# Linear attention gated by an MLP mixer: the first loads in the order in which the products take them up, and other planner settings

## The chip, the cores and the metric

The kernel runs on one core of one Trainium2 chip. The metric is the device time of one execution in microseconds; the median of the runs is compared. TensorE is called PE in the profile, VectorE DVE, ScalarE ACT, GpSimd POOL, and SyncE, which here issues most of the DMAs, SP.

## The reference

x is a 2048x512 float32 matrix (one batch). Its layer norm feeds two branches, and the output is x + s*g:

```python
xn = layernorm(x)
# A: linear attention, H = 32 heads of 16
q, k, v = heads(xn @ wqkv)
phi = lambda t: where(t > 0, t + 1, exp(t)) + 1e-6
pq, pk = phi(q), phi(k)
kv  = einsum("bhsd,bhse->bhde", pk, v)
z   = einsum("bhsd->bhd", pk)
o   = einsum("bhqd,bhde->bhqe", pq, kv) / (einsum("bhqd,bhd->bhq", pq, z)[..., None] + 1e-6)
s   = o.reshape(B, S, D) @ wo
# B: spatial-shift mixer and MLP, D = 512, F = 1376
h  = gelu(layernorm(xn) @ w1)
hs = (four quarters of h's columns, shifted by +1, -1, +2, -2 tokens) @ w2
x1 = xn + hs
g  = silu(x1 + gelu(layernorm(x1) @ w3) @ w4)
out = x + s * g
```

## The kernel before

**Arithmetic.** Nearly every float32 product is split: an operand a is written as a_h + a_l, each of a 32-bit type that PE takes at one pass (fp32r), and a product becomes three matmuls, a_h b_h, a_l b_h and a_h b_l. The ending h or l in a tile's name says which part it is. ACT makes the high part (a copy with a conversion), DVE the low part (a subtraction). A few small products are done as slow float32 matmuls. The weights of the key and query projections have their mean over the rows taken out; the sums for that are the tiles wkt and wqt, and ksum and wqm are the products with ones that come out of them.

**Stages.** x is cut into 16 row blocks of 128 tokens (x0, x1, ...; the tile's name in the profile is x) and, transposed, into 4 blocks of 512 tokens of four 128-row chunks each (xt, whose split parts are u). The first stage projects keys (k, weights wk) and queries (q, weights wq) of a block of 512 tokens. For each row block, sums of x and of its squares (sq, sx, mv on ACT and DVE), a chain of four small POOL operations (w, rs, ns, nm), the normalized x on ACT, and the nonlinearity of k (kt, kr on ACT and DVE, k0h its high part) lead to the Gram products g<-k0h,x0h, which gather keys and values over all tokens. Further stages mix the tokens, then go through the MLP in four blocks of 512 tokens (products into pb, pe, acc), with the attention (products s<-m_b..,q0h), a gate and the output after each block. The products of the mixer and the MLP are arranged in a scheme with seven products in place of eight.

**Order.** A class `Plan` records every operation with its engine, a duration, its tiles and its predecessors. The helpers that record are `mm` (line L146 in the profile), `act` (L167), the DVE and POOL helpers (L189, L194, L199), `load` (L205), `store` (L210), `fetch` (L217) and `gather` (L223, an accumulating DMA on the POOL queue). So all matmuls of the kernel have one line, and an operation is told by its tiles. `emit` then writes one order of instructions for each engine, by a list scheduling over the durations of a model:

- `deadlines` gives the PE operations nominal times in the order in which they were recorded. `backward` walks back from consumers to producers: a producer is due when its earliest consumer is, less a gap and its own duration; for a DMA the duration is an allowance of 6.0 us plus 4 us per MB.
- An operation that reads PSUM off PE is due at its own earliest time plus `PATIENCE` at the latest.
- `nudged` moves single operations ahead: the table `SOONER` lists pairs of an operation's number and a count of quarter microseconds. The operations 19 to 37 are among the first loads and their conversions.
- `emit` takes, among the ready operations of an engine, the one that is due first. `lead` bounds how early a buffer of a pool may be taken before its operation is due (pool "w" holds weights), `window` how far PE may run ahead of its nominal order, and `ahead` the same for a product that opens a new PSUM buffer.

The order is then fixed: an instruction waits on semaphores for its inputs, and everything behind it on its engine waits too. DMAs that SP issues share eight completion semaphores, so SP's ninth DMA waits for the landing of its first.

Of the kernel before, what the change touches and what calls it, by code (L numbers as in the profile page):

```python
# [85 lines left out]
class Plan:  # L86
# [138 lines left out]


    GAP = .06
    PATIENCE = 5.0
    COLD, COLD_TILL = 1.84, 5.8
    SAFE = 2.0  # L230
    early = 0.0
# [8 lines left out]
    def deadlines(self, first):  # L240
# [8 lines left out]
        for op in self.ops:  # L249
# [3 lines left out]
            elif any(t.psum for t in op.tiles):  # L253
                op.due = min(op.due, op.at + self.PATIENCE)
            elif op.soon:
# [5 lines left out]
    def backward(self):  # L261
        for op in reversed(self.ops):
            if op.eng != "PE":
                for o in op.post:
                    op.due = min(op.due, o.due - self.GAP - (6.0 + op.mb * 4 if op.mb else op.lat))

    def emit(self, first, lead, reserve, window, ahead, table=()):
        self.deadlines(first)
# [125 lines left out]
def linear_attn_gated_by_mixer(  # L394
# [43 lines left out]
    pl = Plan(nc, pools, counts, ("acc", "mm"))  # L438
# [904 lines left out]
    for b in range(NQ):  # L1343
# [50 lines left out]
        else:  # L1394
# [17 lines left out]
                gate(b * QT + QT - 1, a, o, D // 2, late=True, by_dma=False, whole=o > 0)  # L1412

    SOONER = (
# [5 lines left out]
    )  # L1420
    pl.emit(first=6.0, lead={"p": 12.0, "w": 10.0, "ab": 10.0}, reserve={"p": 20, "w": 1, "ab": 0}, window=6.0,
            ahead=6.0, table=SOONER)


# [35 lines left out]
```

## Time and profile before

| | |
|---|---|
| median of 3 runs | 521.98 us (521.84 to 522.37) |
| profiled execution | 522.82 us |
| its span in the trace | 520.8 us |
| PE busy | 513.3 us (99%) |
| DVE, ACT, POOL busy | 375.4, 330.7, 110.5 us |
| granted clock of PE | 1.0 throughout |
| HBM traffic | 60.33 MB read, 30.81 MB written |
| chain that ended last | PE 90%, ACT 3%, DMA 3%, DVE 2% |

The profiled execution is 2.02 us longer than its span, and 0.84 us above the median. Rows of the timeline give the start in us from the beginning of the span, the duration, the engine, the helper's line, the operation, the tiles (out<-in, without their buffer numbers), the shapes, and in brackets the idle time before the instruction with what ended it. Durations of matmuls overlap, so PE's pace is read from the distance between starts. A row of SPq is the issue of a DMA, not its transfer. Rows of waits give the total, the number and the longest.

### The profile page before, as it was taken

The numbers are of one execution on the slowest core, as the hardware profiler recorded it, in microseconds if no ns is written. First come the engines' busy times: TensorE is split into PE (matmuls) and PEld (weight loads), VectorE is DVE, ScalarE is ACT, GpSimd is POOL, SyncE is SP. The second block draws the span as 40 slices with busy tenths as digits, with TensorE's granted clock in tenths as the row PEclk, the third lists the DMA queues.
The fourth block names the chain that finished last, engine by engine and source line by source line (L and its number), as shares of the span: only waits on it lengthen the run. The fifth ranks groups of instructions, "written<-read, shape, count | busy, mean of one in ns | idle before, by whom it ended". The sixth has DMA issues, their size and how long they took to land.

```text
span 520.8 us, 8908 instructions
## 1 busy us (share of the span) xinstructions
PE 513.3 (99%) x3017; PEld 446.4 (86%) x3017; DVE 375.4 (72%) x746; ACT 330.7 (63%) x667; POOL 110.5 (21%) x207
## 2 busy tenths in 40 slices
PE   8999999999999999999999999999999999999996
PEld 6777888988888888898999889899898898999985
DVE  4975787668555847999997558896668767695635
ACT  5799884578757858769766656366563456545621
POOL 2478313330463032212000022000140000320000
PEclk9999999999999999999999999999999999999999
DMA  7939993374897279999765769748399465797704
GB/s 269 276 85 203 241 246 79 81 164 141 171 246 188 82 170 247 247 244 264 260 234 188 223 172 225 249 155 192 110 183 299 147 198 129 158 288 232 282 2 119
DMA packets 73281, 100.12 MB, mean 192 GB/s; under 512 B 7844, under 2 KB 30900, under 8 KB 73236
## 3 DMA queue, kind: packets, MB, share of 16 engines
q1 hardware_dynamic: 62148, 79.37, 48.6%
q0 software_dynamic: 11088, 20.19, 23.4%
q8 instruction: 23, 0.38, 0.3%
q14 instruction: 22, 0.18, 0.1%
HBM read 60.33 MB, written 30.81 MB: 175 GB/s over the span
## 4 chain that ended last, share of the span: by engine, by line
PE 90%; ACT 3%; DMA 3%; DVE 2%; issue 0%; SPq 0%; POOL 0%; POOLq 0%; DVEq 0%
PE acc L146 22%; PE pb L146 10%; PE h L146 9%; PE g L146 8%; PE k L146 7%; PE q L146 7%; PE pe L146 5%; PE pbm L146 4%; PE pbs L146 3%; PE pa L146 2%; PE pem L146 2%; PE s L146 2%; PE pes L146 2%; PE a L146 2%; DMA xo<-x1d 2%; PE pam L146 1%
## 5 line engine op out<-in xcount | busy, mean ns | idle before, releaser
L223 POOL DMA_DIRECT2D xo<-x1d x12 | 10.7, 1158 | 168.5 <-ACT xo L167 114.0
L223 POOL DMA_DIRECT2D o<-x x16 | 14.5, 904 | 62.2 <-DVE o L189 44.0
L223 POOL DMA_DIRECT2D th<-in_x x14 | 12.2, 934 | 71.3 <-DVE th L199 57.7
L167 ACT ACTIVATE p<-pb 128x256 f32<-128x256 f32 x20 | 7.7, 384 | 26.3 <-PE pb L146 25.9
L223 POOL DMA_DIRECT2D pqd<-qe x16 | 14.4, 899 | 40.7 <-ACT qe L167 23.4
L199 DVE SCALAR_TENSOR_TENSOR kr<-kt,kr 128x512 f32<-128x512 f32 x16 | 11.1, 691 | 14.5 <-ACT kt L167 14.5
L167 ACT ACTIVATE gf<-gf 128x256 f32<-128x256 f32 (+1 forms) x40 | 20.9, 523 | 0.9
L199 DVE SCALAR_TENSOR_TENSOR kt<-wneg,mv,k 128x512 f32<-128x512 f32 x16 | 11.9, 746 | 10.1 <-PE k L146 9.9
L223 POOL DMA_DIRECT2D zacc<-kr x16 | 15.2, 949 | 14.0 <-DVE kr L199 8.5
L167 ACT ACTIVATE th<-xo 128x512 f32<-128x512 f32 (+1 forms) x16 | 9.6, 615 | 13.1 <-DVE xo L189 11.8
L167 ACT ACTIVATE ht<-ht 128x512 f32<-128x512 f32 x16 | 9.8, 629 | 12.4 <-DVE ht L189 12.4
L189 DVE TENSOR_TENSOR ht<-h,abc 128x512 f32<-128x512 f32 x16 | 10.8, 686 | 8.8 <-PE h L146 6.7
L189 DVE TENSOR_TENSOR gf<-pa,p 128x256 f32<-128x256 f32 x20 | 8.4, 421 | 11.0 <-PE pa L146 5.4
L167 ACT ACTIVATE p<-pe 128x256 f32<-128x256 f32 x20 | 7.6, 381 | 12.9 <-PE pe L146 12.9
L167 ACT ACTIVATE x<-x,nm,rs 128x512 f32<-128x512 f32 x16 | 12.3, 804 | 5.5 <-POOL nm L189 5.5
L167 ACT ACTIVATE y<-o,nm,rs 128x512 f32<-128x512 f32 x16 | 11.9, 805 | 3.8 <-POOL nm L194 3.8
L590 DVE BATCH_NORM_STATS2 st<-o 128x6 f32<-128x512 f32 x16 | 11.0, 686 | 4.6 <-DMA o<-x 4.6
L189 DVE TENSOR_TENSOR gf<-u,pe 128x256 f32<-128x256 f32 x20 | 8.3, 415 | 7.8 <-PE pe L146 7.8
L167 ACT ACTIVATE qe<-q,ns 128x512 f32<-128x512 f32 x16 | 10.9, 679 | 4.6 <-PE q L146 4.5
L167 ACT ACTIVATE kr<-kt,rs 128x512 f32<-128x512 f32 x16 | 11.5, 716 | 2.7 <-DVE kt L199 2.7
L199 DVE SCALAR_TENSOR_TENSOR qz<-pq,zb 128x512 f32<-128x512 f32 x16 | 10.8, 681 | 2.6 <-PE acc L146 2.6
L199 DVE SCALAR_TENSOR_TENSOR th<-th,so 128x512 f32<-128x512 f32 (+1 forms) x17 | 10.9, 657 | 2.2 <-ACT th L167 1.6
(1569 smaller groups left out, 2190.7 us busy)
## 6 DMA issues: line engine op xcount, KB each, us to landing
w_s<-in_w SPq DMA_DIRECT2D x28, 256.0 KB, 6.2
x<-in_x SPq DMA_DIRECT2D x16, 256.0 KB, 4.9
zacc<-kr POOLq DMA_DIRECT2D x16, 256.0 KB, 5.4
pqd<-qr SPq DMA_DIRECT2D x16, 256.0 KB, 3.0
pqd<-qe POOLq DMA_DIRECT2D x16, 256.0 KB, 5.0
o<-x POOLq DMA_DIRECT2D x16, 256.0 KB, 5.4
x1d<-o SPq DMA_DIRECT2D x16, 256.0 KB, 3.7
pq<-pqd SPq DMA_DIRECT2D x16, 256.0 KB, 3.8
```

The costliest lines, as they stand in the source:

```text
L146: lambda: nc.tensor.matmul(out.get(), lhs.get(), rhs.get(), start=start, stop=stop, skip_group_check=more))
L167: nc.scalar.activation(out.get(), src.get(), func, scale=get(scale), **kw)
L189: self.vec(eng, out, [a, b], lambda: self.e(eng).tensor_tensor(out.get(), a.get(), b.get(), op=op), True)
L199: lambda: self.nc.vector.scalar_tensor_tensor(out.get(), a.get(), get(s), b.get(), op0=op0, op1=op1),
L223: lambda: self.nc.gpsimd.dma_start(out.get(), get(src), accum_op=ALU.add), mb=mb)
L590: pl.add("DVE", .62, .69, [xv], [st], lambda: nc.vector.bn_stats(st.get(), xv.get()))
```

## The change

The same operations are recorded, and only the planner's settings differ: `PATIENCE` is halved, the DMA allowance in `backward` falls from 6.0 to 4.0 us, `window` is doubled, `ahead` falls from 6.0 to 4.0, the lead of the weight pool grows from 10 to 14, and the table `SOONER` is another one, with large entries for the first loads.

```diff
-    PATIENCE = 5.0
+    PATIENCE = 2.5
...
-                    op.due = min(op.due, o.due - self.GAP - (6.0 + op.mb * 4 if op.mb else op.lat))
+                    op.due = min(op.due, o.due - self.GAP - (4.0 + op.mb * 4 if op.mb else op.lat))
...
     SOONER = (
-        19, 6218, 23, 5332, 27, 842, 30, 870, 34, 216, 36, 863, 40, 23, 42, 842, 44, 606, 45, 153, 129, 10,
-        137, 641, 139, 89, 143, 41, 183, 55, 185, 178, 187, 92, 189, 92, 191, 14, 362, 5, 625, 6, 632, 15,
...
+        19, 13683, 20, 10270, 21, 8588, 23, 12463, 26, 10287, 28, 89, 29, 8809, 31, 9, 32, 8315, 34, 248,
+        35, 9622, 37, 16, 42, 972, 44, 621, 45, 262, 55, 85, 83, 60, 91, 24, 93, 19, 129, 21, 137, 828, 139, 77,
...
     )
-    pl.emit(first=6.0, lead={"p": 12.0, "w": 10.0, "ab": 10.0}, reserve={"p": 20, "w": 1, "ab": 0}, window=6.0,
-            ahead=6.0, table=SOONER)
+    pl.emit(first=6.0, lead={"p": 12.0, "w": 14.0, "ab": 10.0}, reserve={"p": 20, "w": 1, "ab": 0}, window=12.0,
+            ahead=4.0, table=SOONER)
```

Each engine runs as many instructions as before. The new orders differ in about 95 rows on PE, 226 on DVE, 145 on ACT, 36 on POOL and 83 on SP, most of them moved by a few places. The first loads on SP:

| place | before | after |
|---|---|---|
| 1 | wk, chunk 0 (256 KB) | wk, chunk 0 |
| 2 | xt chunk 0, first half (128 KB) | xt chunk 0, first half |
| 3 | xt chunk 0, second half (128 KB) | xt chunk 1 |
| 4 | xt chunk 2 (256 KB) | wk, chunk 1 |
| 5 | wk, chunk 1 (256 KB) | xt chunk 0, second half |
| 6 | xt chunk 1 (256 KB) | xt chunk 2 |
| 7 | x0 (256 KB) | wk, chunk 2 |
| 8 | wk, chunk 2 (256 KB) | xt chunk 3 |
| 9 | xt chunk 3 (256 KB) | x0 |
| 10 | wk, chunk 3 (256 KB) | wk, chunk 3 |

On PE the products of chunk 1 for the first two row blocks come right behind the float32 ones of chunk 0; on ACT two second passes of sq (row blocks 2 and 3) stand ahead of k1h, and qe and qr of the first row blocks behind k2h. The last 60 rows of PE are the same in both.

7 rows, old and new, of the table SOONER are left out of this document.

## The prediction

> **What bounds the kernel now.** I read the page first, then what PE waits for, then the busy time by stretch, then single instructions where PE is not full.
>
> ```profile
> PE 513.3 (99%) x3017; PEld 446.4 (86%) x3017; DVE 375.4 (72%) x746; ACT 330.7 (63%) x667; POOL 110.5 (21%) x207
> ...
> PE k L146 <- ACT u_1h L167: 0.7, 1, 0.7
> PE g L146 <- ACT k2h L167: 0.4, 1, 0.4
> ...
> 5.00:10.00 5.00, 4.18 (x13) 2.51 (x14) 3.13 (x6) 3.00 (x7) 0.00 (x0) 1.00 0.92 312
> ...
> 30.00:40.00 10.00, 9.57 (x42) 7.48 (x41) 6.58 (x17) 9.87 (x19) 7.82 (x15) 1.00 0.43 102
> ```
>
> The first line says that TensorE is busy in 513.3 of 520.8 us. The next two are the longest waits in the middle of its work, both in the first 40 us. The stretches confirm it: PE lacks 0.82 us between 5 and 10 and 0.43 us between 30 and 40, and in the second of these it is ACT that is full (9.87 of 10). The change issues the same operations, so PE's work stays as it is, and only the places where PE stands still, or runs at less than its pace, can give or cost time. PE's order is a single queue, so whatever it loses at one place stays lost unless a later wait absorbs it.
>
> ```profile
> 8.28 0.40 PE L146 MATMUL k<-wk_0h,u_0l 128*128 128x512 f32 x1
> 9.42 0.50 PE L146 MATMUL k<-wk_1h,u_1h 128*128 128x512 f32 x1 [0.74 <-ACT u_1h L167]
> ...
> 20.00 0.73 PE L146 MATMUL g<-k0h,x0h 128*128 128x512 f32 x2
> ...
> 29.30 0.40 PE L146 MATMUL q<-wq_1h,u_1h 128*128 128x512 f32 x1
> 29.54 1.20 PE L146 MATMUL g<-k1h,x1h 128*128 128x512 f32 x4
> ...
> 35.20 0.40 PE L146 MATMUL q<-wq_1l,u_1h 128*128 128x512 f32 x1
> 36.02 1.20 PE L146 MATMUL g<-k2h,x2h 128*128 128x512 f32 x4 [0.43 <-ACT k2h L167]
> ```
>
> A 512-wide product takes PE one step of about 0.23 us (29.30 to 29.54 is 0.24; the longer durations of the rows overlap). By that step three places can be priced: 8.28 to 9.42 is 1.14, less 0.23 makes 0.91 us lost for u_1h; 35.20 to 36.02 is 0.82, less 0.23 makes 0.59 us lost for k2h; 29.30 to 29.54 loses nothing.
>
> **The first loads.** The change swaps the order on SP. Before: weight chunk 0, two halves of token chunk 0, token chunk 2, weight chunk 1, token chunk 1, row block x0, weight chunk 2, token chunk 3. After: weight chunk 0, half of token chunk 0, token chunk 1, weight chunk 1, the other half, token chunk 2, weight chunk 2, token chunk 3, and x0 only as the ninth.
>
> ```profile
> 7.37 0.33 SPq L205 DMA_DIRECT2D wq_s<-in_wqkv  x1
> 8.73 0.33 SPq L205 DMA_DIRECT2D x<-in_x  x1
> 9.35 0.33 SPq L205 DMA_DIRECT2D wq_s<-in_wqkv  x1
> ...
> 11.12 0.33 SPq L205 DMA_DIRECT2D x<-in_x  x1
> ```
>
> SP has eight loads under way and issues another when the one eight places back has landed, so its late issues date the landings: the issue at 7.37 dates the fifth load (weight chunk 1), at 8.73 the sixth (token chunk 1), at 9.35 the seventh (x0), at 11.12 the ninth (token chunk 3). All carry 256 KB but the two halves of 128 KB, and I take it that a load lands when as many bytes have come in ahead of it as before. Token chunk 1 is then complete with 640 KB in place of 1280 KB, well before 7.37 and not at 8.73; weight chunk 1 with 896 KB in place of 1024, some 0.7 us sooner (estimate: half of the 1.36 us between 7.37 and 8.73 that 256 KB took). x0 comes ninth, so it lands at about 11.1 in place of 9.35: 1.8 us later. PE's order follows: products of chunks 0 and 1 first, in the order in which they come.
>
> The 0.91 us for u_1h go. What is late next: the second half of chunk 0, which now comes fifth and lands where weight chunk 1 did, at about 7.4; weight chunk 1's conversion on ACT; and the sum over the weights, whose last addition on DVE now stands behind x0's row sums. I give the waits for them 0.2 us each, 0.6 in all (bounds 0.3 and 1.0). The first 45 products come out ahead by 0.3 us.
>
> **Row block 0.** g<-k0h at 20.00 is the first consumer of a chain that begins with x0.
>
> ```profile
> 9.36 0.64 ACT L167 ACTIVATE sq<-x 128x512 f32<-128x512 f32 x1
> ...
> 14.42 0.81 ACT L167 ACTIVATE x<-x,nm,rs 128x512 f32<-128x512 f32 x1 [1.73 <-POOL nm L189]
> ...
> 17.00 0.71 ACT L167 ACTIVATE kr<-kt,rs 128x512 f32<-128x512 f32 x1
> ...
> 19.22 0.72 ACT L167 ACTIVATE k0h<-kr,tiny 128x512 fp32r<-128x512 f32 x1 [0.76 <-DVE kr L199]
> ...
> 25.50 0.62 ACT L167 ACTIVATE u_0h<-xt 128x512 fp32r<-128x512 f32 x1
> 26.02 0.73 ACT L167 ACTIVATE kr<-kt,rs 128x512 f32<-128x512 f32 x1
> ...
> 28.78 0.71 ACT L167 ACTIVATE k1h<-kr,tiny 128x512 fp32r<-128x512 f32 x1
> 29.39 0.71 ACT L167 ACTIVATE sq<-x,sx 128x512 f32<-128x512 f32 x1
> 30.10 0.71 ACT L167 ACTIVATE sq<-x,sx 128x512 f32<-128x512 f32 x1
> ...
> 35.26 0.71 ACT L167 ACTIVATE k2h<-kr,tiny 128x512 fp32r<-128x512 f32 x1
> ```
>
> ```profile
> 11.40 0.62 POOL L194 TENSOR_SCALAR w<-mv 128x1 f32<-128x1 f32 x1 [8.35 <-DVE mv L194]
> ...
> 13.91 0.47 POOL L189 TENSOR_TENSOR nm<-mv,ns 128x1 f32<-128x1 f32 x1
> ...
> 25.08 0.24 POOL L194 TENSOR_SCALAR w<-mv 128x1 f32<-128x1 f32 x1 [3.70 <-DVE mv L194]
> ...
> 26.61 0.19 POOL L189 TENSOR_TENSOR nm<-mv,ns 128x1 f32<-128x1 f32 x1
> ```
>
> From sq at 9.36 to the normalized x at 14.42 the chain took 5.06 us, of which four tiny POOL operations took 11.40 to 14.38, 2.98 us. The same four for the next rows took 25.08 to 26.80, 1.72 us. With x0 at 11.12, x is normalized from about 16.2 at the long price and from 14.9 at the short one. Before, kr could start only at 17.00, and x ends by 17.0 even at the long price, so the chain of x0 eats its slack but hardly passes it. The change also puts x0h behind kr and kt on ACT, which takes one conversion out of the way of k0h (0.52 us, 25.50 to 26.02). g<-k0h comes between 19.2 (short price: x0h's 0.52 and PE's lead of 0.3 both tell) and 20.1 (long price: kr at 17.0 as before); I take 19.6, near the middle, since nothing in the trace of before has these operations beside each other: 0.4 us ahead.
>
> A page of the Trainium skill speaks against the short price: "SBUF — State Buffer", section "Who interferes with whom", says that a VectorE instruction with two inputs in SBUF and a GpSimd instruction that reads SBUF shut each other out for the whole instruction. By it the long price would hold, because VectorE's order in the changed kernel has such instructions (the weight sums, the low halves) all through this stretch. The two stretches of POOL rows are what the rule would give; that the first ran beside such VectorE work I take as the cause, but no run shows it yet. I make it a rival below.
>
> **Row blocks 1 and 2.** On ACT two second passes of the row sums (sq of blocks 2 and 3) move from behind k1h to ahead of it, u_0h of the next tokens moves from ahead of it to later, and kr, kt, x, x2h, k2h follow k1h directly, with the q conversions (qe, qr) behind them.
>
> k1h is pushed back by 2 x 0.71 and pulled forward by u_0h's slot (25.50 to 26.02, 0.52): 0.90 us later, less the 0.4 by which row block 0 is ahead. It starts at 29.28, ends at 29.99, and g<-k1h starts at 30.0. PE by then has two more q products behind it (2 x 0.23 = 0.46), which makes 30.0 worth 29.54: the gain up to here is nil, and a new wait of some 0.4 us for k1h shows. From k1h's start to k2h's ACT then takes what kr to k1h took, 28.78 - 26.02 = 2.76, and a slot of k1h more (0.61), so k2h is ready at about 33.4. g<-k2h stands five q products earlier, at 36.02 - 0.59 - 5 x 0.23 = 34.3 plus nothing gained: its wait of 0.59 us goes, with 0.9 us to spare. The conversions of q that are now later must be read before their PSUM is wanted again; they are three, at the 0.6 us of an ACT slot, and I see no PE product that waits; if one did, it would cost some tenths. The start gives **0.6 us** (bounds 0.0 and 1.0).
>
> **The rest.** The other parameters (smaller patience for PSUM readers, a shorter allowance for DMA, a different window) leave PE's order unchanged over long stretches and the last 60 products as they are, and shift about 95 of 2959 PE rows in all. They act where one accumulator must be read before the next product may write it.
>
> ```profile
> 244.40 0.63 PE L146 MATMUL acc<-w_10h,f_10h 96*128 96x512 f32 x2
> ...
> 245.15 0.39 PE L146 MATMUL pb<-yt40h,w_b 128*128 128x256 f32 x1
> ...
> 245.97 0.28 PE L146 MATMUL s<-m_b11h,q0h 128*128 128x256 f32 x1
> ...
> 296.08 0.40 PE L146 MATMUL acc<-w_3h,f_3l 128*128 128x512 f32 x1
> 296.31 0.36 PE L146 MATMUL pb<-yt40h,w_b 128*128 128x256 f32 x1
> 296.51 0.28 PE L146 MATMUL pb<-yt40l,w_b 128*128 128x256 f32 x1
> ```
>
> At 244.40 two products should end their steps at 244.86, but pb starts at 245.15: 0.29 us lost. The changed order has more products between the two, so that goes. At 296.31 the step is 0.20 where a 256-wide one takes half of 0.23, so 0.08 is lost; of this small kind the new order fills six places and opens four, 0.2 us in favour. Against that, the rows s<-m_b11h at 245.97 are moved some 2.4 us up, to about 243.4, and ACT's and DVE's work for them must be there sooner; I put 0.2 us for new waits there (bounds 0 and 2, next part). The rest: -0.29 - 0.16 + 0.2 = **-0.25 us** (bounds -0.6 and +0.3).
>
> **Sum.** The profiled execution took 522.82 (span 520.8 and 2.02 around it). 522.82 - 0.6 - 0.25 = 521.97. The median of the runs, 521.98, is 0.84 below that execution; the same steps from it give 521.13, which I round to **521.1 us**. A change of 0.2%, 1.04 us, is about what a measurement of this kernel can tell from none; mine is 0.85.
>
> **The rivals.**
>
> ```profile
> 225.84 1.83 POOL L223 DMA_DIRECT2D o<-x  x2 [9.87 <-PE kv L146]
> ...
> 233.41 1.93 SPq L217 DMA_DIRECT2D q0t<-q0d  x4
> ...
> 236.20 0.94 SPq L210 DMA_DIRECT2D x1d<-o  x2
> ...
> 241.61 0.64 ACT L167 ACTIVATE q0h<-q0t 128x512 fp32r<-128x512 f32 x1
> ```
>
> *Slower: the fetch of q0t caught behind a store.* In SP's new order the four fetches of q0t stand behind the store x1d, which must wait until the gather o<-x has landed; before, they stood ahead of it. The gathers go out at 225.84, and nothing of SP's would pass a late one. From the fetch at 233.41 to the first use at 241.61 lie at most 8.2 us, with q0h's 0.64 some 8.9 to a product; s wanted at 243.4 asks for a fetch by 234.5. Each us after that costs PE one. To be slower by 1.04 after a gain of 0.85 the fetch must go out at 236.4, near where x1d went before (236.20). Against it: the gather has from 226 to 234 for 256 KB. For it: these are the transfers with the fullest DMA. At 236.9 it gives 521.1 + 2.4 = 523.5.
>
> *Little gained: row block 0 becomes the bound.* The long price of the POOL chain holds, g<-k0h stays at 20.0, k1h is not pulled ahead by 0.4, g<-k1h comes at 30.4, and the start gives 0.2: 521.98 - 0.2 - 0.25 = 521.5. The skill's rule on the shared port would bring this case.
>
> *Faster by more.* The short price holds and ACT is 0.8 us ahead at k0h, so k1h costs nothing and the start gives 1.0; the turn-arounds give 0.5 with no new wait: 521.98 - 1.5 = 520.5.
>
> **How the numbers follow.** The forecast of 521.1 gets 0.52, and being 0.16 from the bound of 520.94 I put 0.20 of it on the faster side; faster by more gets 0.17; row block 0 as the bound 0.13; the slower case 0.18. Faster by over 0.2%: 0.20 + 0.17 = 0.37. Within 0.2%: 0.32 + 0.13 = 0.45. Slower by over 0.2%: 0.18. The likeliest case's own range is 520.7 to 521.6. The range that holds 8 in 10 reaches from 520.2 (start 1.0, rest 0.6, and a little) to 523.0, just into the slower case.
>
> **What would show it.** Right: no wait of PE for u_1h, a new one of about 0.4 us for k1h at 30, none for k2h, g<-k3h some 0.6 us earlier than at 40.5; sq of x0 on ACT at 11.1; no gap ahead of pb at 245. Wrong: x0 landing before 10.5 (loads not taken in bytes and order), g<-k0h after 20.1, a PE wait for q conversions between 33 and 45, PE waiting for q0h or a fetch near 243, or a wait behind 260 that before does not have.

## The result: 0.4% slower, and the profile after

The changed kernel takes **523.98 us** (median of 5, 523.54 to 525.05), the kernel before in the same session 522.29 (5 runs, 521.84 to 522.37). The ratio is 1.0039 [1.0028, 1.0050]: slower by 1.7 us by the medians and 2.0 by the ratio, above the upper end of the range (523.0) and on the other side from the forecast of 521.1.

The profiled execution of after took 523.54 (span 521.5). That is as short as the fastest of its five runs, while the profiled one of before, 522.82, lies above all five timed runs of before in that session. One pair of traces therefore shows less than the medians, and I profiled the same changed kernel a second time (e4_after_again: 525.77, span 523.7).

The page and the waits of PE in the first profile of after:

```profile
PE 514.0 (99%) x3017; PEld 445.9 (85%) x3017; DVE 377.1 (72%) x746; ACT 328.2 (63%) x667; POOL 112.2 (22%) x207
...
PE ksum L146 <- DVE wkt L189: 0.5, 1, 0.5
PE k L146 <- ACT wk_1h L167: 0.3, 1, 0.3
PE g L146 <- ACT k1h L167: 0.2, 1, 0.2
PE g L146 <- ACT k0h L167: 0.2, 1, 0.2
...
PE pe L146 <- ACT p L167: 0.2, 1, 0.2
```

The waits for u_1h and k2h are gone, as the change meant them to. Four small ones have come in their place at the start, and one far behind it: pe waits for ACT's p. The stretches say the same. The first line is before's, between 10 and 15, and the others are after's:

```profile
10.00:15.00 5.00, 5.00 (x22) 3.68 (x20) 4.71 (x12) 3.05 (x7) 2.73 (x4) 1.00 1.03 386
```

```profile
5.00:10.00 5.00, 4.70 (x16) 2.79 (x17) 3.13 (x6) 2.62 (x6) 0.00 (x0) 1.00 0.96 311
10.00:15.00 5.00, 4.50 (x17) 2.84 (x16) 4.22 (x10) 3.83 (x9) 1.28 (x2) 1.00 1.00 371
...
30.00:40.00 10.00, 9.77 (x42) 7.54 (x41) 7.76 (x16) 9.87 (x16) 7.04 (x13) 1.00 0.45 106
```

PE gains 0.52 us between 5 and 10 and 0.20 between 30 and 40, and now stands still for 0.50 us between 10 and 15, which is the wait for wkt.

PE runs 3017 products in both kernels, so the two traces can be laid beside each other, the n-th product of one with the n-th of the other (about 95 of them differ in order, by a few places). The table gives, for each stretch of the kernel (by the times of before), how much PE falls behind within it, against the first profile of before, in us. Negative is a gain.

| profile | 0-40 | 40-73 | 73-98 | 98-253 | 253-430 | 430-460 | 460-515 | in all |
|---|---|---|---|---|---|---|---|---|
| after, first | -0.08 | 0.06 | 0.22 | -0.20 | -0.04 | 0.54 | 0.25 | 0.75 |
| after, second (e4) | -0.09 | 0.06 | 1.20 | -0.26 | -0.06 | 0.60 | 1.52 | 2.97 |
| before, second (e13) | -0.05 | -0.01 | 0.02 | -0.05 | -0.29 | 0.02 | 0.00 | -0.36 |

The two profiles of before agree within 0.36 us. The two of after lose time in the same three places, near 75, near 452 and near 490, by amounts that differ from run to run. None of the three is at the start, and at each of them PE waits for something that hangs on a DMA.

**Place 1, near 75.** SP's order around the last four weight loads for the mixer (w2), before and then the first profile of after:

```profile
47.61 2.80 SPq L205 DMA_DIRECT2D w_s<-in_w  x4
51.60 0.33 SPq L210 DMA_DIRECT2D pqd<-qr  x1
```

```profile
47.80 2.31 SPq L205 DMA_DIRECT2D w_s<-in_w  x3
51.18 0.34 SPq L210 DMA_DIRECT2D pqd<-qr  x1
...
52.20 0.55 SPq L205 DMA_DIRECT2D w_s<-in_w  x1
```

Before, all four are out by 50.41, and the store of qr, which must wait for ACT to make qr, comes behind them. After, the last load stands behind that store and goes out at 52.20. Its first reader on DVE is w_f. Before, the first profile of after, and the second, each with DVE's k7l that comes later in the same queue, and with PE's first product that needs k7l:

```profile
58.56 0.69 DVE L189 TENSOR_TENSOR w_f<-w_s,w_s 128x512 f32<-128x512 f32 x1
...
73.81 0.69 DVE L199 SCALAR_TENSOR_TENSOR k7l<-kr,k7h 128x512 fp32r<-128x512 f32 x1 [0.19 <-ACT k7h L167]
...
74.83 0.40 PE L146 MATMUL g<-k7l,x7h 128*128 128x512 f32 x1
```

```profile
59.95 0.69 DVE L189 TENSOR_TENSOR w_f<-w_s,w_s 128x512 f32<-128x512 f32 x1 [0.15 <-DMA w_s<-in_w]
...
74.14 0.69 DVE L199 SCALAR_TENSOR_TENSOR k7l<-kr,k7h 128x512 fp32r<-128x512 f32 x1
...
74.89 0.51 PE L146 MATMUL g<-k7l,x7h 128*128 128x512 f32 x1
```

```profile
60.94 0.69 DVE L189 TENSOR_TENSOR w_f<-w_s,w_s 128x512 f32<-128x512 f32 x1 [1.14 <-DMA w_s<-in_w]
...
75.13 0.68 DVE L199 SCALAR_TENSOR_TENSOR k7l<-kr,k7h 128x512 fp32r<-128x512 f32 x1
...
75.86 0.50 PE L146 MATMUL g<-k7l,x7h 128*128 128x512 f32 x1 [0.49 <-DVE k7l L199]
```

Before, k7l ends at 74.50, only 0.33 us ahead of its use. From there to the first profile of after w_f is 1.39 us later and k7l only 0.33, so slack behind w_f takes up the rest. Between the two profiles of after w_f differs by 0.99 us, k7l by 0.99 and the product by 0.97: the wait on DVE for the load goes through 14 us of DVE's queue, here one to one, and comes out on PE. In the waits of PE it has the name k7l, and nothing there names the load.

**Place 2, near 452.** The rows of xo are brought in by four gathers that POOL issues (L223). Before, and then the first profile of after, with ACT and PE:

```profile
445.03 3.54 POOL L223 DMA_DIRECT2D xo<-x1d  x4 [54.50 <-DMA w_5l<-w4d]
450.07 0.63 ACT L167 ACTIVATE th<-xo 128x512 f32<-128x512 f32 x1
```

```profile
445.07 3.53 POOL L223 DMA_DIRECT2D xo<-x1d  x4 [54.03 <-ACT xo L167]
451.33 0.63 ACT L167 ACTIVATE th<-xo 128x512 f32<-128x512 f32 x1 [1.15 <-DMA xo<-x1d]
451.86 0.37 ACT L167 ACTIVATE p<-pe 128x256 f32<-128x256 f32 x1
...
451.74 0.39 PE L146 MATMUL acc<-w_10h,f_10h 96*128 96x512 f32 x1
452.28 0.39 PE L146 MATMUL pe<-yb223h,w_s1h 128*128 128x256 f32 x1 [0.15 <-ACT p L167]
```

ACT waits 1.15 us for xo, and p, which empties the PSUM that PE wants next, is queued behind th. From 451.74 to 452.28 are 0.54 us, less one step of 0.23: 0.31 lost here, and the rest of the stretch's 0.54 comes in small steps behind it. The order on ACT is the same in before, and the gathers go out at the same time; but th starts 6.3 us after the first of them, in before 5.0. What differs beside them is SP: in after two of its DMAs go out between the gathers, at 446.02 and 446.44, in before none. Over all eighteen profiles (the experiments below among them) this goes together: in the seven with two SP DMAs there (after, e4 to e8, e10) ACT waits for xo, 0.2 to 1.8 us at a time, and in the eleven with one or none it doesn't. That the neighbours on SP make the gathers land late is a reading of these profiles; no run moved them alone.

**Place 3, near 490.** The fetch of q14t on SP, in before and then in the first profile of after:

```profile
474.36 1.78 SPq L217 DMA_DIRECT2D q14t<-q14d  x4
```

```profile
481.92 2.05 SPq L217 DMA_DIRECT2D q14t<-q14d  x4
...
488.99 0.63 ACT L167 ACTIVATE q14h<-q14t 128x512 fp32r<-128x512 f32 x1 [1.12 <-DMA q14t<-q14d]
```

It goes out 7.6 us later, behind the fetch of xo and four of w4. In the first profile ACT just makes it. In the second it does not:

```profile
491.45 0.63 ACT L167 ACTIVATE q14h<-q14t 128x512 fp32r<-128x512 f32 x1 [2.64 <-DMA q14t<-q14d]
491.99 0.36 ACT L167 ACTIVATE p<-pb 128x256 f32<-128x256 f32 x1
...
491.75 0.28 PE L146 MATMUL pa<-yb213h,w_al 128*128 128x256 f32 x1
492.40 0.39 PE L146 MATMUL pb<-yt23h,w_s0h 128*128 128x256 f32 x1 [0.38 <-ACT p L167]
493.20 0.38 PE L146 MATMUL pe<-yt13h,w_s0h 128*128 128x256 f32 x1 [0.41 <-ACT so L167]
```

The products start 0.65 and 0.80 us apart, where a 256-wide product takes a step of 0.12 (half of 0.23): 1.2 us lost.

### The profile page after: what moved, and what is told of

The parts are those of the page before. It is cut to its first block, busy times and chain, and to the rows that moved or that the text cites. A ratio compares the mean times of both kernels' runs of the same rounds, so it can differ in the third digit from the quotient of the medians.

```text
span 521.5 us, 8875 instructions
## 1 busy us (share of the span) xinstructions
PE 514.0 (99%) x3017; PEld 445.9 (85%) x3017; DVE 377.1 (72%) x746; ACT 328.2 (63%) x667; POOL 112.2 (22%) x207
## 4 chain that ended last, share of the span: by engine, by line
PE 88%; issue 4%; DVE 3%; DMA 2%; ACT 2%; SPq 0%; POOLq 0%; DVEq 0%; ACTq 0%
PE acc L146 21%; PE pb L146 11%; PE h L146 9%; PE g L146 8%; PE q L146 7%; PE k L146 6%; PE pe L146 5%; PE pbm L146 4%; PE pbs L146 3%; PE pa L146 3%; PE pem L146 2%; PE s L146 2%; PE a L146 2%; PE pes L146 1%; DMA wk_s<-in_wqkv 1%
## 5 line engine op out<-in xcount | busy, mean ns | idle before, releaser
L223 POOL DMA_DIRECT2D xo<-x1d x12 | 10.7, 1172 | 166.7 <-ACT xo L167 108.7
L223 POOL DMA_DIRECT2D th<-in_x x14 | 12.1, 906 | 73.3 <-DVE th L199 63.2
L223 POOL DMA_DIRECT2D o<-x x16 | 13.9, 869 | 52.2 <-DVE o L189 43.7
L223 POOL DMA_DIRECT2D pqd<-qe x16 | 15.7, 1002 | 33.9 <-ACT qe L167 21.5
L223 POOL DMA_DIRECT2D zacc<-kr x16 | 15.7, 983 | 29.0 <-DVE kr L199 17.1
L167 ACT ACTIVATE gf<-gf 128x512 f32<-128x512 f32 (+1 forms) x40 | 20.8, 521 | 0.7
L189 DVE TENSOR_TENSOR f_10l<-gf,f_10h 96x512 fp32r<-96x512 f32 x4 | 2.7, 687 | 17.7 <-ACT gf L167 12.7
L167 ACT ACTIVATE qr<-q,rs 128x512 f32<-128x512 f32 x16 | 10.8, 676 | 1.7 <-POOL ns L194 1.7
```

Of the source, the lines that this page charges most:

```text
L167: nc.scalar.activation(out.get(), src.get(), func, scale=get(scale), **kw)
L189: self.vec(eng, out, [a, b], lambda: self.e(eng).tensor_tensor(out.get(), a.get(), b.get(), op=op), True)
L223: lambda: self.nc.gpsimd.dma_start(out.get(), get(src), accum_op=ALU.add), mb=mb)
```

## The experiments

In most of them the order of instructions was written out. The planner's call is replaced by one that issues the recorded operations in a given list, so that any stretch can follow the one or the other kernel:

```diff
-    pl.emit(first=6.0, lead=..., reserve=..., window=..., ahead=..., table=SOONER)
+    pl.forced(first=6.0, order=list(zip(ISSUED, ISSUED_AT)), table=SOONER)
```

Each was timed beside the kernel before on its chip, whose medians were 522.08 to 522.19.

**Which stretch of the new order costs.** The list follows the one kernel up to a given product on PE, with all that the other engines do until then, and the other kernel from there.

```diff
 e1
+ISSUED = after's up to product 400 (about 94 us), before's from there
 e2
+ISSUED = after's up to product 2121 (about 380 us), before's from there
 e3
+ISSUED = before's up to product 2500 (about 437 us), after's from there
 e4: the changed kernel again, no edit
```

> The operations are issued in the changed kernel's order up to the 400th product of PE (about 94 us) and in the order of before from there on. Theory A (the start gives nothing and costs nothing: what the new first loads win, x0's later landing and the two sq passes ahead of k1h take back): within 0.3 us of before; by the trace of after PE stands 0.05 to 0.2 us behind before at this point. Theory B (the first loads are what makes the changed kernel slower): 1.2 to 2 us slower than before.

> The order of after up to the 2121st product (about 380 us), that of before from there on. Theory A (the loss comes late): 0.2 to 0.6 us slower than before, as far as the trace of after is behind there. Theory C (the loss is spread over all stages in proportion to the moved rows): 1.2 to 1.6 us slower.

> The order of before up to the 2500th product (about 437 us), that of after behind it. Theory A (ACT and SP queues of the last block let PE wait for gathers and fetches, and for longer in some runs than in the profiled one): 0.8 to 1.8 us slower than before, with runs that differ by more than those of before do. Theory B or C: under 0.4 us.

> The changed kernel unchanged, for a second profiled execution and more times. All theories: 1.3 to 2.2 us slower than before. Theory A: where this profile is longer than the first one, the difference lies behind 437 us, at a wait that ends with a DMA; theory C: it is spread.

| kernel | median | ratio to before |
|---|---|---|
| e1 | 522.52 | 1.0008 [1.0000, 1.0017] |
| e2 | 523.09 | 1.0013 [1.0005, 1.0022] |
| e3 | 523.54 | 1.0023 [1.0014, 1.0032] |
| e4 | 524.15 | 1.0039 [1.0027, 1.0052] |

The start gains nothing: with the stretch to 94 us in the new order the kernel is rather slower. The end alone, which has nothing of the first loads, costs 1.37 us (523.54 - 522.17). The three parts, 0.35 for e1, 1.37 for e3 and 0.25 for the stretch between them (e15 below), add up to 1.97, and e4 is 1.98 above before. That the two agree to 0.01 is luck: each part has an interval of about 0.45 us either way, and e2, which has the new order up to 380 us, lies 0.92 above before by its median, where e1 and e15 together make 0.60. It is enough to say that most of the loss is not the price of the new start.

**Each of the three places undone**, in the order of after:

```diff
 e5, SP near 480
-q15t x4, xo, w4 x4, q14t x4
+q15t x4, q14t x4, xo, w4 x4
 e6, ACT near 452
-p<-pb, th<-xo, p<-pe, u<-pb
+p<-pb, p<-pe, u<-pb, th<-xo
 e7, SP near 47 (qr2, qr3, qr4 are stores of qr, w1 and w2 loads)
-qr2, qr3, w1 x4, arow, w2 x3, qr4, arow, w2 x1
+qr2, w1 x3, qr3, w1 x1, arow, w2 x4, qr4, arow
 e8: all three
```

> The changed kernel with one move: SP issues the four fetches of q14t ahead of the fetch of xo12 and of four weight loads, five places sooner. Theory A (in the last block ACT's q14h waits for this fetch, and the readers p and so of PSUM queue behind it, for which PE waits: 0 us in the first profile of the changed kernel, 1.2 us in the second): 0.4 to 0.9 us faster than the changed kernel, so 1.1 to 1.6 us slower than before, and no wait of PE for p or so near 492. Theory D (the late loss is DMA traffic as such, whatever its order): no change against the changed kernel, 1.7 to 2.2 us slower than before.

> The changed kernel with one move on ACT: th8, which waits for the landing of the gather xo8, behind the two readers p and u that follow it near 452 (and the DVE operation on th8 with it). Theory A: the 0.31 to 0.40 us that PE lost ahead of pe<-yb223h go, 1.4 to 1.8 us slower than before. Theory D: no change, 1.7 to 2.2 us slower.

> The changed kernel with two moves on SP between 35 and 52 us, as before had it: the store of qr3 behind the third of the first four weight loads, and the next four weight loads ahead of the store of qr4. Theory A (in the changed kernel the last of these loads lands at 59.9 to 60.9 us, DVE's w_f stands in front of the work for row block 7 and waits for it, and PE loses 0.1 to 1.0 us at g<-k7h and g<-k7l): 0.2 to 0.6 us faster than the changed kernel, 1.3 to 1.8 us slower than before, no wait of PE for k7. Theory D: no change.

> The changed kernel with the moves of the three runs above together. Theory A: 1.0 to 1.8 us faster than the changed kernel, so 0.2 to 1.0 us slower than before; runs differ by less than those of the changed kernel. Theory D: 1.7 to 2.2 us slower than before.

| kernel | median | ratio to before | stretch, in its profile |
|---|---|---|---|
| e5 | 523.75 | 1.0027 [1.0016, 1.0039] | 460-515: 0.20 |
| e6 | 524.06 | 1.0035 [1.0021, 1.0048] | 430-460: 0.60 |
| e7 | 522.40 | 1.0007 [0.9998, 1.0017] | 73-98: 0.03 |
| e8 | 522.26 | 1.0004 [0.9995, 1.0013] | 73-98: 0.05; 460-515: 0.19 |

e7 moves a few DMA issues on SP by some places and takes most of the loss away, far more than the 0.2 to 0.6 us that were expected of it. Its profile shows the chain of place 1 whole again, in the same views as above:

```profile
47.11 2.77 SPq L205 DMA_DIRECT2D w_s<-in_w  x4
...
59.00 0.68 DVE L189 TENSOR_TENSOR w_f<-w_s,w_s 128x512 f32<-128x512 f32 x1
...
73.83 0.40 PE L146 MATMUL g<-k7h,x7h 128*128 128x512 f32 x1
74.06 0.40 PE L146 MATMUL g<-k7l,x7h 128*128 128x512 f32 x1
```

No wait on DVE, and a step of 0.23 on PE. In the six profiles that have after's order here, with the last w2 load behind the store (both of after, e1, e2, e5, e6), DVE waits 0.15 to 1.14 us for it, and the stretch 73-98 loses 0.22 to 1.20 us, 0.86 in the mean. In e7 and e8, with the loads ahead, it loses 0.03 and 0.05. The order of load and store is not the whole condition, though: e10 (below) has the load behind the store and loses 0.28, because w_f stands later on DVE, and e14 and e16 have it ahead and lose 0.56 and 0.33, because PE is earlier.

e7 moved two things, the store qr3 behind the third w1 load and the last w2 load ahead of the store qr4; which of them counts wasn't separated. Nor does its gain fit with e3 by simple addition. e3 says that the end alone costs 1.37 us, and e7 keeps that end: its own profile loses 0.27 at place 2 and 0.89 at place 3, yet its median is only 0.2 above before. In that profile the start is 0.8 us ahead and the stretch 98-430 another 0.7, which offsets the loss there. The intervals leave room for about 0.9 us at place 1 and about 0.8 at the end, and no run narrows that.

e5 moves the fetch of q14t ahead, and 0.20 us is left of a mean of 0.83 over five profiles that have it late (0.25, 1.52, 0.54, 0.90, and 0.92 in e3). Its median agrees in direction, but its interval overlaps that of after. Nor is the fetch all of this stretch: e9 (below) has the same order on SP here and loses 0.28, while e1 and e2, which have before's, lose 0.35 and 0.44 at a product near 483. e6 failed: p no longer waits for th, but DVE's th, which kept its place, now waits 1.08 us for ACT's, gf is queued behind it, and pb waits 0.4 us for gf at 455. The stretch stays at 0.60. It is xo that is late, and moving its first reader only moves the wait.

**Which setting does it.** Three builds by the planner, with single settings exchanged:

```diff
 e9, in after:
-                    op.due = min(op.due, o.due - self.GAP - (4.0 + op.mb * 4 if op.mb else op.lat))
+                    op.due = min(op.due, o.due - self.GAP - (6.0 + op.mb * 4 if op.mb else op.lat))
 e10, in before:
-                    op.due = min(op.due, o.due - self.GAP - (6.0 + op.mb * 4 if op.mb else op.lat))
+                    op.due = min(op.due, o.due - self.GAP - (4.0 + op.mb * 4 if op.mb else op.lat))
 e11, in before: the new table's entries for the operations 19 to 37, the old ones for all others
```

> The changed kernel with the DMA allowance in backward put back from 4.0 to 6.0 us and all else as changed; the planner then issues the last load of w2 ahead of the store of qr4 again, as before did. Theory E (the shorter allowance is the part of the change that costs: it makes loads due later, so SP puts stores ahead of them): PE loses nothing at k7, 0.8 to 1.5 us faster than the changed kernel, so 0.2 to 1.2 us slower than before. Theory F (the loss comes with the first loads or the new table): 1.5 to 2.2 us slower than before.

> The kernel before with that allowance alone cut to 4.0 us; the stores of qr3 and qr4 then stand ahead of weight loads on SP as in the changed kernel. Theory E: DVE waits for the load near 60, PE loses 0.6 to 1.2 us at k7, 0.6 to 1.8 us slower than before. Theory F: within 0.4 us of before.

> The kernel before with only the entries of the new table for the first loads (operations up to 37), the rest of the old table and all other settings as before. Theory E: the start wins 0.1 to 0.9 us as in the profiles of the changed kernel and nothing is lost later, 0.1 to 0.9 us faster than before. Theory F: 0.5 to 2 us slower.

| kernel | median | ratio to before |
|---|---|---|
| e9 | 523.56 | 1.0026 [1.0015, 1.0037] |
| e10 | 524.11 | 1.0045 [1.0031, 1.0060] |
| e11 | 526.48 | 1.0077 [1.0064, 1.0089] |

In e10 the shorter DMA allowance alone, with before's start, costs 2.0 us by the medians. Its SP order at 47 is that of after (three w2 loads, the store, the fourth behind it, here at 57.61). But its w_f stands later on DVE, at 68.02, and doesn't wait for the load, so that place 1 costs it 0.28 us and not the 0.6 to 1.2 that I had expected. Its profile has waits of PE that before's does not have, at other places:

```profile
PE pb L146 <- DVE gf L189: 0.6, 1, 0.6
PE pem L146 <- ACT p5m L167: 0.4, 1, 0.4
```

p5m stands on a full ACT queue behind the conversion of a weight (it starts at 223.26, in before at 222.38), and gf on a full DVE queue behind splits of q12, near 484; neither shows a wait for a DMA.

e9 restores the order of the w2 loads (73-98: 0.00 in its profile) but keeps 1.4 us of loss, which its profile, the fastest of its runs, does not show. So the allowance alone is enough to cost as much as was lost, by another route than place 1, and taking it back does not give most of the loss back.

e11 shows that the new first loads do not stand alone. Without the settings around them PE waits for k0h at 20.79:

```profile
PE g L146 <- ACT k0h L167: 1.7, 1, 1.7
```

The span of its profile, the fastest of its runs, is 2.2 us longer than that of the first one of before, and only 0.64 of that is there by 40 us; its median is 4.3 us above before. Where the rest goes is open.

**A better start by hand.** In the order of before, token chunk 1 and weight chunk 1 are loaded ahead of token chunk 2, second passes of sq fill a gap on ACT, and conversions of q go behind k2h (e12), or behind k3h, with kr of block 2 ahead of four row statistics on DVE (e14). e13 is the kernel before as a run of its own, for the spread. e15 is before with after's middle (products 400 to 2500), e16 the start of e14 with that middle.

```diff
 e12, e14, e16, SP
-wk0, xt0a, xt0b, xt2, wk1, xt1, x0, wk2
+wk0, xt0a, xt0b, xt1, wk1, xt2, x0, wk2
```

> The order of before with two repairs by hand: the load of token chunk 1 and that of weight chunk 1 ahead of that of token chunk 2 (x0 stays seventh), with u_1 ahead of u_2 on ACT and DVE; and the second sq passes of blocks 2 and 3 put into the gap in which ACT waits ahead of wq_3h (1.52 us in before), with the POOL chain behind them, the first q conversions behind k2h. If the two gaps of before (0.91 us for u_1h, 0.59 us for k2h) are what bounds the start: 0.7 to 1.4 us faster than before. If the chain of row block 0 takes over whatever comes sooner: 0.3 to 0.7 us faster (the second gap alone).

> The kernel before unchanged, for a second profiled execution. The first one, 522.82 us, was 0.7 us above the median of all its runs. If its 0.91 us for u_1h and 0.59 us for k2h are there in the usual run too, PE reaches g<-k3h at 40.0 to 40.6 us again; if the usual run loses less there, it does so 0.5 us or more sooner, and then the start of the changed kernel wins nothing against it.

> The order of before with the first loads as in the run with two gaps closed, the second sq passes of blocks 2 and 3 in ACT's gap ahead of wq_3h, and the conversions of q0 and q1 behind k3h in place of k2h, with DVE's kr of block 2 ahead of four row sums of the next blocks. If the last 0.67 us that the earlier run lost at k3l were due to the conversions ahead of k3h: 0.3 to 1.0 us faster than before. If the start is bound by x0 and the POOL chain in the usual run: within 0.3 us of before.

> The order of before up to product 400 (94 us), that of the changed kernel from there to product 2500 (437 us), then that of before again. If the turn-arounds of PSUM are what the middle of the change wins (0.25 us at 245 by both profiles of the changed kernel, nothing in sum behind it): 0.1 to 0.5 us faster than before. If the middle costs too: 0.3 us slower or more.

> The start by hand of the run above, the middle of the changed kernel, the end of before. If both add up: 0.4 to 1.5 us faster than before, and faster than both kernels. If not: within 0.3 us of before.

| kernel | median | ratio to before | PE against before, after 40 us | after 98 us |
|---|---|---|---|---|
| e12 | 522.75 | 1.0009 [1.0001, 1.0018] | -1.16 | -0.46 |
| e13 | 522.09 | 1.0000 [0.9989, 1.0010] | -0.05 | -0.04 |
| e14 | 522.55 | 1.0009 [1.0000, 1.0018] | -1.11 | -0.48 |
| e15 | 522.33 | 1.0007 [0.9998, 1.0016] | -0.28 | -0.29 |
| e16 | 522.44 | 1.0010 [1.0001, 1.0019] | -1.19 | -0.80 |

The hand-made starts do win 1.1 us by 40 us in their profiles, and 0.4 to 0.7 of it is gone by 98. In e14 PE waits for k7l, as at place 1, though the w2 loads are ahead of the store:

```profile
73.48 0.69 DVE L199 SCALAR_TENSOR_TENSOR k7l<-kr,k7h 128x512 fp32r<-128x512 f32 x1 [0.19 <-ACT k7h L167]
...
74.23 0.51 PE L146 MATMUL g<-k7l,x7h 128*128 128x512 f32 x1 [0.22 <-DVE k7l L199]
```

PE is a microsecond earlier here, but k7l only 0.33 (73.48 against 73.81), so PE waits for it. k7l starts right behind ACT's k7h, as it does in before, and a late load isn't what holds it. In e12 it is g<-k3l, which waits for DVE near 40 (0.67 lost between 40 and 73). No version is faster than before by its median. e16's profile ends 1.21 us ahead of the first one of before (the second of before, 0.36), but it is the fastest of its eleven runs (521.49 to 523.46); where the others lose that lead isn't shown.

## Why the prediction was wrong, step by step

**The failed step is in "The rest":** that the other settings leave PE's order unchanged over long stretches and so shift little. The order of the products does stay nearly the same (about 95 of 3017 change places), but what mattered were DMA issues. Of the 83 moved rows on SP I followed, behind the start, only those near 233, where the fetch of q0t is, and put the others at nothing. Loads and fetches slip behind stores and other transfers, and ACT and DVE wait for them with PSUM readers and splits queued behind; e7, which moves SP issues and nothing else, brings the ratio from 1.0039 to 1.0007. The term was set at -0.25. From the profiles it is -0.26 (98-253), -0.16 (253-430, with e13 at -0.29 a spread of the same size), +0.86 at place 1, +0.61 at place 2 and +0.83 at place 3: +1.9.

**The rival on the slower side had the mechanism and the wrong place.** A transfer caught behind a store is what happens at 52 (a weight load behind a store of qr), and at 482 one is caught behind other fetches. At the place that I named it costs nothing: the fetch of q0t goes out at 231.77, ahead of the 234.5 that I had asked for, and s<-m_b11h starts at 243.87 without a wait.

**The gap ahead of pb at 245 goes,** as forecast, and the wait set against it doesn't come: the stretch 98-253 gains 0.20 to 0.32 in the six profiles with all of after's order there.

**The start, right in its causes and too high in its sum.** PE, ACT and DVE of the first profile of after:

```profile
12.33 0.40 PE L146 MATMUL k<-wk_2l,u_2h 128*128 128x512 f32 x1
13.22 1.13 PE L146 MATMUL ksum<-wkt,ones 128*128 128x512 f32 x2 [0.50 <-DVE wkt L189]
...
20.21 0.97 PE L146 MATMUL g<-k0h,x0h 128*128 128x512 f32 x3 [0.23 <-ACT k0h L167]
...
30.63 0.97 PE L146 MATMUL g<-k1h,x1h 128*128 128x512 f32 x3 [0.23 <-ACT k1h L167]
...
11.25 0.63 ACT L167 ACTIVATE sq<-x 128x512 f32<-128x512 f32 x1
...
16.10 0.82 ACT L167 ACTIVATE x<-x,nm,rs 128x512 f32<-128x512 f32 x1 [0.51 <-POOL nm L189]
...
12.49 0.68 DVE L189 TENSOR_TENSOR wkt<-wkt,wk_s 128x512 f32<-128x512 f32 x1
```

- x0's sq starts at 11.25; 11.1 was forecast. Loads taken in bytes and order held.
- The wait for k1h (30.00 to 30.63, less 0.23: 0.40) is the 0.4 forecast, and none for k2h is left.
- ksum waits 12.33 to 13.22, less 0.23: 0.66 us, where I had put 0.2. The cause is the one named, wkt behind x0's row sums on DVE, but it starts only at 12.49.
- g<-k0h comes at 20.21, not at 19.6 and just above the bound of 20.1.

In all the start gives 0.08 us in both profiles of after and 0.36 in the mean of the eight profiles with this order (0.97 to -0.14), in place of 0.6. The rival "row block 0 becomes the bound" is what these eight show. x0's sq starts at 10.31 to 11.48 in them, g<-k0h follows 8.9 to 9.0 us behind it, g<-k1h 10.4 behind that and g<-k3h 9.8 behind that, so what x0's landing gains or loses PE gains or loses almost in full: 0.97 ahead with 10.31, 0.14 behind with 11.48. From x0 at 11.1 to g<-k0h at 19.6 the prediction allowed 8.5 us, and this step is the one that was sized too small. Where the profile of e6 comes out with nearly the forecast figures (19.58, 30.00, a gain of 0.71), it is because x0's sq starts at 10.61 there, half a microsecond ahead of the forecast: luck. The chain of row block 0 on POOL, in the first profile of after:

```profile
13.64 0.60 POOL L194 TENSOR_SCALAR w<-mv 128x1 f32<-128x1 f32 x1 [10.58 <-DVE mv L194]
...
15.73 0.33 POOL L189 TENSOR_TENSOR nm<-mv,ns 128x1 f32<-128x1 f32 x1
...
25.30 0.23 POOL L194 TENSOR_SCALAR w<-mv 128x1 f32<-128x1 f32 x1 [3.28 <-DVE mv L194]
...
26.88 0.19 POOL L189 TENSOR_TENSOR nm<-mv,ns 128x1 f32<-128x1 f32 x1
```

It takes 13.64 to 16.06, 2.42 us, between the short price (1.72 in before, 1.77 here for the next rows) and the long one (2.98). The Trainium skill's page "SBUF — State Buffer", section "Who interferes with whom", says that such POOL work and two-input DVE work shut each other out. The chain is longer than the short price, as it would be by that rule, but DVE has a two-input row beside the short chain near 26 too, and no run here took the DVE work away, so the trace doesn't settle it.

**And what the start wins is not carried.** I let a gain at the start stand to the end unless a later wait absorbs it, and named none. The k7 chain at 74.8, with 0.33 us to spare, is such a wait (e14), and in e12 it is g<-k3l.

**The sum by the profiles:** -0.36 + 0.06 + 0.86 - 0.26 - 0.16 + 0.61 + 0.83 = +1.6 us, against +1.7 and +2.0 by the medians. It is a sum of means over single executions that differ by up to a microsecond at each place, and it counts from the first profile of before, a slow one; from the second it would be about +2.0. e7 and e8 hold up place 1, and e5 place 3 in its profile. Place 2 is seen in the six profiles of after, e4 to e8 (0.27 to 1.11), but no run took it away, and why the gathers land late is argued and not shown. Open are the rest in e9 and in e11, how the loss divides among the places, and why e7 takes off 1.5 to 1.7 us by its median where its place loses 0.86 in the profiles (the interval, about 0.8 either way, allows both).

## What to carry to other kernels

When a planner's setting for DMAs changes, list every load, fetch and store that changes places on its queue, and for each the first instruction that reads it and what stands behind that reader; PE's own order may stay nearly as it is and still lose 1.6 us (after against e7). A wait on an engine travels down its in-order queue, and what slack doesn't absorb on the way comes out on PE, here 15 us later and under another name: of the 1.39 us at w_f 0.33 were left at k7l, and of the 0.99 more in the second profile all of it. Before pricing a gain, look for the next place where PE's slack is only a few tenths: it caps what an earlier start can bring.

## What the runs showed of the hardware

The same transfer, issued at the same time in the same program, lands up to 1 us later from one execution to the next: in the two profiles of after the last w2 load is issued at 52.20 and 52.22, and DVE's reader starts at 59.95 and 60.94. The landing of x0, 10.31 to 11.48 by its reader, moved PE at 40 us by nearly the same amount. A fetch with little margin is then a cost by chance, 0.0 in one run and 1.2 in another (q14t), and one profile may show neither. Profiles of an identical order up to 40 us were apart there by 1.1 us (-0.97 to 0.14), as far as the effects that were being looked for.
